# A circular 7x7 convolution kernel: pixel transfers of the head merged and reordered, forward jobs by halves, two weight jobs ahead of the first round

## The chip, the cores and the metric

The kernel runs on one core of a Trainium2 chip. The metric is the time of one execution on the device in microseconds (us); the median of several runs counts. TensorE (PE in the profile) multiplies matrices, PEld is its weight load, VectorE is DVE, ScalarE is ACT, GpSimd is POOL, and SyncE (SP) issues most of the DMA transfers.

## The reference

```python
x: (1, 224, 224, 96) bfloat16, w: (7, 7, 96, 96) bfloat16
wp = jnp.pad(w, ((0, H - K), (0, W - K), (0, 0), (0, 0)))
Xf = jnp.fft.rfft2(x.astype(jnp.float32), axes=(1, 2))
Wf = jnp.fft.rfft2(wp.astype(jnp.float32), axes=(0, 1))
Yf = jnp.einsum('bhwi,hwio->bhwo', Xf, Wf)
y = jnp.fft.irfft2(Yf, s=(H, W), axes=(1, 2)).astype(jnp.bfloat16)
```

This is a circular convolution over the image: each output pixel depends on its own row and the 6 above it and on its own column and the 6 to the left of it, wrapping around at the edges, and all 96 channels mix.

## The kernel before

The kernel cuts the image's 224 rows into 8 strips of 28 and takes each strip, with the 6 rows above it, through a short real transform over its rows; the result stands in 17 slots (`NS = 17`) of two numbers each. Along the columns it works directly, with seven taps shared between even and odd pixels. Four strips, with 6 rows above them, make a row block of 118 rows (`R = HB + PAD`); there are two row blocks, `jg` 0 and 1. The columns are cut into 7 tiles of 32 pixels.

The stages are these:

- Weights. `wqx` holds the weights with the taps on partitions. `prep_jobs(gi)` transforms one group of slots (`PGRP`) in 12 jobs of four matmuls each; each job fills a PSUM bank and is evicted into `WF`. Group 0 covers slots 0 and 1, group 1 slots 2 to 4; after its 12 jobs follow three VectorE differences (`diff`), so group 1 has 15 jobs.
- Forward. `f_jobs(t, s0, s1)` transforms the pixels of tile `t` for slots `s0` to `s1`. For the first eight slots of tile 0 there are four jobs for each row block: pixels 0 to 15, even and odd, then pixels 16 to 31, even and odd. Each job is eight matmuls of 64 columns into one bank, evicted as 512 columns into `xf`. The six wrap-around pixels at the right edge of the image (`xh_bufs`) go through `a_bank`, three matmuls of 136 columns a job.
- Rounds. `jit` forms sums and differences of `xf` on VectorE (the planes `J`), and `b_round(t, s, mid, end, ...)` multiplies them with `WF`. Inside a round, `mid` and `end` run waiting jobs of the queues `qs` (weights of later groups, forward jobs of later slots and tiles). `add(a, b, jobs)` spreads a list of jobs evenly over the half-rounds `a` to `b`, and `pace` says how many are due.
- The back transform of the output comes later and is not touched.

`evac` chooses the engine of each eviction by a planner: two running sums, `load["v"]` for VectorE and `load["a"]` for ScalarE, with an estimated cost for each eviction; the one with the smaller sum takes it. Just before the first round the sums are set to `BIAS` = 2000 and 0.

All engines run their instructions in the order in which the program issues them (`_Ordered`). SyncE's order in the head is six weight transfers, then ten pixel transfers: for each row block the wrap-around pixels (112 rows, then the 6 rows above, which wrap around), and then for each row block the pixels of tile 0 in three parts: first half of 112 rows, all pixels of the 6 wrap rows, second half of 112 rows. The first half is `TW * C + 32` = 1568 elements wide. The buffers lie in the last eight slots of `WF` (`late`), so that the profile shows these transfers as `WF<-in_x_dram`.

In program order the head is: group 0 of the weights, wrap-around pixels of both row blocks, eight forward jobs, the second tile's pixel transfers (which wait for the eviction of the fifth of the eight jobs, `last[-4]`), `jit(0, 0)`, and the rounds.

Of the kernel before, what the change touches and what calls it, by code (L numbers as in the profile page):

```python
# [21 lines left out]
PAD = KT - 1  # L22
Q = 2 * LC
MAGIC = 12582912.0
TW = 16
# [7 lines left out]
PGRP = ((0, 2), (2, 5), (5, 8), (8, 11), (11, 14), (14, 17))  # L33
# [11 lines left out]
MERGE = ()  # L45
NP2 = 0
FI = 6
LROUND = {8: 16, 11: 15}
WARM0 = 2
YLATE = {(0, 3): 0, (0, 4): 1}  # L50
BIAS = 2000.0


def slot(s, part):
    return part if s == 0 else 2 + 3 * (s - 1) + part
# [3 lines left out]
def kernel(  # L59
# [7 lines left out]
    _, H, W, C = x.shape  # L67
# [3 lines left out]
    HB = JG * B  # L71
    R = HB + PAD
# [36 lines left out]
    def bank():  # L109
        return pools["psb"].tile([128, 512], F32, name="pb")  # L110

    load = {"v": 0.0, "a": 0.0}
# [3 lines left out]
    def apart(key, zone, r):  # L116
        for z, q in parts.setdefault(key, []):
            if z != zone and q.engine != r.ins.engine:
                tc.declare_no_dep(r.ins, q, reason="disjoint parts of one tile")
        parts[key].append((zone, r.ins))  # L120
        return r

    def evac(out_ap, in_ap, n):
        if tail[0]:
            return tail_evac(out_ap, in_ap, n)
        cv, ca = 180 + 1.0 * n, 160 + 0.85 * n
        if load["v"] + cv <= load["a"] + ca:
            load["v"] += cv
            return VE.tensor_copy(out=out_ap, in_=in_ap)
        load["a"] += ca  # L130
        return SE.copy(out=out_ap, in_=in_ap)
# [5 lines left out]
    def dma(out_ap, in_ap):  # L137
        return DE.dma_start(out=out_ap, in_=in_ap)
# [11 lines left out]
    XW = 2 * TW * C  # L150
# [11 lines left out]
    XHW = PAD * C + 32  # L162
    late = WF[0:R, NSLOT - 8:NSLOT].rearrange("p a t o -> p (a t o)")
    x0_bufs = [late[:, i * (XW + 32):(i + 1) * (XW + 32)] for i in range(2)]
    xh_bufs = [late[:, 2 * (XW + 32) + i * XHW:2 * (XW + 32) + (i + 1) * XHW] for i in range(2)]
    assert 2 * (XW + 32 + XHW) <= 8 * NTAP * C and NSLOT - 8 > slot(PGRP[-1][0], 0)

    def load_rows(xb, jg, w0, npx, cut=0):
        h0 = jg * HB - PAD
        n = npx * C  # L170

        def ld(p0, p1, hh, c0=0, c1=n):
            return dma(xb[p0:p1, c0:c1], x[0, hh:hh + (p1 - p0), w0:w0 + npx, :].rearrange("h w c -> h (w c)")[:, c0:c1])
        if cut:
            return ld(PAD, R, h0 + PAD, 0, cut), ld(0, PAD, h0 % H), ld(PAD, R, h0 + PAD, cut, n)
        return ld(PAD, R, h0 + PAD), ld(0, PAD, h0 % H)
# [13 lines left out]
    def apart_w(r, rows=None, cols=None):  # L190
        for pr, pc, d in beside:
            if cols is not None and pc is not None and cols != pc or rows is None or pr is None or not rows & pr:
                tc.declare_no_dep(r.ins, d.ins, reason="other columns or rows")
        beside.append((rows, cols, r))
# [4 lines left out]
    for c, (c0, c1) in enumerate(cuts):  # L199
        apart_w(dma(wqx[up:up + lr, c0:c1], wsrc[0:lr, c0:c1]), {1, 2}, c)  # L200
        apart_w(dma(wqx[QD:up, c0:c1], wsrc[lr + QD - up + 1:lr + 1, c0:c1]), {-1}, c)
    for jg in range(2):
        load_rows(xh_bufs[jg], jg, W - PAD, PAD)
    for jg in range(2):
        load_rows(x0_bufs[jg], jg, 0, 2 * TW, TW * C + 32)

    def shift(eng, q, c):
        o, i = halves((q + 2) % 4, c, 0), halves(q, c, C2)
# [7 lines left out]
    def warm(n):  # L216
        pwu = bank()
        for _ in range(n):
            TE.matmul(pwu[:].rearrange("p (a b) -> p a b", a=4), lhsT=wu[:, 0:128], rhs=wur, start=True, stop=True)
# [62 lines left out]
    for h, r, lo, hi in ((0, 0, up - 1, up - 1 + PW - 1), (1, 0, 0, QD - 1), (1, 1, 2 * QD + up - 1, PW2 - 1)):  # L282
        o = flag[:, h, r:r + 1]
# [31 lines left out]
    for r, n, v in ((0, 0, 1.0), (0, LC, -1.0), (1, 1, -1.0), (1, L - 1, 1.0)):  # L315
        o = mf[:, :, 2 * NS - 2 + r:2 * NS - 1 + r]
# [71 lines left out]
    def prep_jobs(gi):  # L388
        s0, s1 = PGRP[gi]
        ns = s1 - s0  # L390
        full = gi == 0
        ncol = (NSLOT_OF(s0, s1) if full else 2 * ns) * NTAP
        nb = C // NB
        hb = NB // 2
        nr = 512 // NB if full else ncol
        assert ncol <= nr and NB * nr <= 512 and C2 % hb == 0

        def mk_(ob):
            def f():
                pw = bank()  # L400
                pv_ = pw[:, 0:NB * nr].rearrange("p (k h q) -> p k h q", h=2, q=nr)
                ev = Em[:, :, slot(s0, 0):slot(s1 - 1, 2) + 1, :]
                ev = Em.rearrange("p h a t -> p h (a t)")[:, :, 0:nr] if full else ev.rearrange("p h (s r) t -> p h s (r t)", r=3)[:, :, :, 0:2 * NTAP]
                for k in range(hb):
                    o = ob * hb + k
                    TE.matmul(pv_[:, k], lhsT=wqx[0:PW2, o:o + 127 * C + 1:C], rhs=ev, start=True, stop=True)
                pv_ = pv_[0:C]
                o0, o1 = ob * hb, (ob + 1) * hb
                wv = WF[0:C, slot(s0, 0):slot(s1 - 1, 2) + 1]
                if full:  # L410
                    wv = wv.rearrange("i a t (h o) -> i (a t) h o", h=2)
                    apart(("W", gi), ob, evac(wv[..., o0:o1], pv_[..., 0:ncol].rearrange("i k h q -> i q h k"), NB * ncol))
                    return
                wv = wv.rearrange("i (s r) t (h o) -> i s (r t) h o", r=3, h=2)
                apart(("W", gi), ob, evac(wv[:, :, 0:2 * NTAP, :, o0:o1],
                      pv_.rearrange("i k h (s q) -> i s q h k", s=ns), NB * ncol))
            return f

        def diff(s):
            def f():  # L420
                load["v"] += 60 + C * NTAP / 1.92
                w0, w1, w2 = (WF[0:C, slot(s, r)].rearrange("i t o -> i (t o)") for r in range(3))
                VE.tensor_tensor(out=w2, in0=w0, in1=w1, op=ALU.subtract)
            return f
        return [mk_(ob) for ob in range(nb)] + ([] if full else [diff(s) for s in range(s0, s1) if s not in REAL])

    def NSLOT_OF(s0, s1):
        return slot(s1 - 1, 2) + 1 - slot(s0, 0)
# [67 lines left out]
    def f_jobs(t, s0, s1):  # L496
        n = 2 * (s1 - s0) * JG
        nr = -(-TW * n // 512)
        e = [-(-TW * i // nr) for i in range(nr + 1)]
        assert max(b - a for a, b in zip(e[:-1], e[1:])) * n <= 512  # L500
        fv = Fm[:, :, s0:s1].rearrange("p r s j -> p r (s j)")

        def mk_(jg, a, b, ph):
            def f():
                pa = bank()
                for k in range(b - a):
                    i = 2 * (a + k) + ph
                    TE.matmul(pa[:, k * n:(k + 1) * n], lhsT=xbuf(t, jg)[:, i * C:i * C + 128], rhs=fv, start=True, stop=True)
                xo = xf_tiles[t][0:C, ph, :, s0:s1, HALO + a:HALO + b, jg * JG:(jg + 1) * JG]
                pi = pa[0:C, 0:(b - a) * n].rearrange("c (w r s j) -> c r s w j", r=2, s=s1 - s0, w=b - a)  # L510
                return apart(("A", t), (a, jg, ph, s0), evac(xo, pi, (b - a) * n))
            return f
        return [[mk_(jg, a, b, ph) for a, b in zip(e[:-1], e[1:]) for ph in range(2)] for jg in range(2)]
# [307 lines left out]
        for f in a_bank(0, xf0, xh_bufs[jg], 0, 3, jg, 0):  # L821
            f()
    fj = [f_jobs(0, a, b) for a, b in zip(FR0[:-1], FR0[1:])]
    last = [f() for jg in range(2) for f in fj[0][jg]]
    for jg in range(2):
        for d in load_x(1, jg):
            tc.add_manual_dep(d.ins, last[-4].ins.name, SYNC, reason="second tile's pixels later")
# [17 lines left out]
    def fills(qs, k):  # L845
        def f():
            for q in qs:
                pace(q, k)
        return f
# [3 lines left out]
    def add(a, b, jobs):  # L853
        qs.append([a, b, jobs, len(jobs)])

    for gi in range(1, len(PGRP)):
        add(2 * PGRP[gi - 1][0], 2 * PGRP[gi - 1][1] - 1, prep_jobs(gi))
    for t in range(2):
        scr_tiles[t] = dr_pool.tile([TW, NJ, NS, 4 * C], BF16, name="scr")
    bursts = {}  # L860
# [8 lines left out]
    for r in range(NS + LAG):  # L869
# [5 lines left out]
        for p in range(3):  # L875
            if r == (1, 3, 5)[p]:
# [4 lines left out]
                fj = f_jobs(1, SH2[p], SH2[p + 1])  # L881
# [4 lines left out]
        for s0, s1, k0, n in FR2:  # L886
            if 2 * r == k0:
                new_xf(2, s0, s1)
                fj = f_jobs(2, s0, s1)
# [33 lines left out]
    for t in range(2, NT):  # L923
# [19 lines left out]
        for s in range(NS):  # L943
# [8 lines left out]
            mid = fills(qs, 2 * s)  # L952
            if t == TL and s in LROUND:
                now = late_planes(LROUND[s])
            if t == TL and s >= SA:
# [18 lines left out]
    def first(j, h):  # L974
        pc = bank()[0:MO, 0:NC]
        TE.matmul(pc.rearrange("p (w g e) -> p w g e", w=2, e=4), lhsT=GA, rhs=TA[:, 2 * h:2 * h + 2, j], start=True, stop=False)
        return pc
# [7 lines left out]
    warm(WARM0)  # L985
    live = {k: first(*k) for k in order[:FI]}
    LF = 4
    for i, (j, h) in enumerate(order):
# [3 lines left out]
        k = i + 8 - LF  # L992
        if FI <= k < len(order):
            live[order[k]] = first(*order[k])
        if i % 2 == 1:
            w0 = TL * 2 * TW
# [34 lines left out]
```

## Time and profile before

| what | us |
|---|---|
| median of 3 runs (lowest to highest) | 256.68 (256.66 to 256.75) |
| profiled execution, whole time | 257.48 |
| its span, first to last instruction | 255.8 |
| TensorE busy in the span | 246.6 |
| VectorE, ScalarE, GpSimd busy | 215.1, 201.1, 107.9 |
| first matmul of the first round (slot 0) | 16.51 after the span's start |

The granted clock of TensorE is 0.994 of full speed. All times inside the profile are from the span's start. A line of the timeline has start, length, engine, source line, operation, output and inputs, shapes, the number of instructions merged, and in brackets the idle time before it with what ended it. All instructions carry line 92, a helper that records them, so groups are told apart by their tiles and shapes.

### The profile page before, as it was taken

The numbers are of one execution on the slowest core, as the hardware profiler recorded it, in microseconds if no ns is written. First come the engines' busy times: TensorE is split into PE (matmuls) and PEld (weight loads), VectorE is DVE, ScalarE is ACT, GpSimd is POOL, SyncE is SP. The second block draws the span as 40 slices with busy tenths as digits, with TensorE's granted clock in tenths as the row PEclk, the third lists the DMA queues.
The fourth block names the chain that finished last, engine by engine and source line by source line (L and its number), as shares of the span: only waits on it lengthen the run. The fifth ranks groups of instructions, "written<-read, shape, count | busy, mean of one in ns | idle before, by whom it ended". The sixth has DMA issues, their size and how long they took to land.

```text
span 255.8 us, 11924 instructions
## 1 busy us (share of the span) xinstructions
PE 246.6 (96%) x5015; PEld 231.7 (91%) x5015; DVE 215.1 (84%) x463; ACT 201.1 (79%) x499; POOL 107.9 (42%) x174
## 2 busy tenths in 40 slices
PE   8989999999999999999999999999999999999981
PEld 3779999999999999998999989999999999999971
DVE  6999899899888878789688896788978889989881
ACT  7889978484965977987988879988897976567762
POOL 7874514364447535331433324433233332465620
PEclk9999999999999999999999999999999999999997
DMA  7954002811111589997969379697959943595145
GB/s 169 239 155 128 27 26 68 255 42 57 49 49 53 160 221 150 279 318 211 311 172 265 96 202 246 180 266 194 329 203 209 265 160 104 146 176 164 54 128 171
DMA packets 41511, 42.80 MB, mean 167 GB/s; under 512 B 30836, under 2 KB 33072, under 8 KB 41458
## 3 DMA queue, kind: packets, MB, share of 16 engines
q1 hardware_dynamic: 41140, 41.36, 59.1%
q8 instruction: 39, 0.64, 1.1%
q0 software_dynamic: 192, 0.52, 0.7%
q10 hardware_dynamic: 126, 0.17, 0.2%
q14 instruction: 14, 0.11, 0.1%
HBM read 22.37 MB, written 19.66 MB: 164 GB/s over the span
## 4 chain that ended last, share of the span: by engine, by line
PE 87%; DMA 5%; ACT 2%; issue 2%; DVE 1%; SPq 1%; POOL 0%; DVEq 0%
PE pb L92 87%; DMA WF<-in_x_dram 2%; DMA wq<-in_w_dram 2%; SPq L92 1%; ACT xf L92 1%; DVE xf L92 1%; POOL yf L92 0%; ACT tt L92 0%; DVE u L92 0%; DVE v L92 0%; ACT WF L92 0%; ACT ct L92 0%; ACT tt__688 L92 0%; DVEq L92 0%
## 5 line engine op out<-in xcount | busy, mean ns | idle before, releaser
L92 PE MATMUL pb<-WF,J 96*128 96x96 bf16 x2782 | 160.8, 206 | 0.1
L92 PEld LDWEIGHTS <-J 96*128 96x128 bf16 x2782 | 137.0, 98 | 7.0 <-issue 0.2
L92 POOL TENSOR_TENSOR yf<-v,u 128x384 bf16<-128x384 f32 x70 | 69.7, 1010 | 119.6 <-issue 63.2
L92 ACT CAST xf<-pb 96x408 bf16<-96x408 f32 (+8 forms) x145 | 68.1, 492 | 3.8 <-PE pb L92 1.9
L92 PE MATMUL pb<-WF,xf 96*128 96x96 bf16 x991 | 61.5, 206 | 0.9 <-ACT xf L92 0.4
L92 DVE TENSOR_TENSOR J<-xf 96x1824 bf16<-96x1824 bf16 (+1 forms) x82 | 56.0, 722 | 0.1
L92 PEld LDWEIGHTS <-xf 96*128 96x128 bf16 x991 | 48.9, 98 | 1.6 <-issue 0.7
L92 PE MATMUL pb<-Fm,xn 118*128 118x136 bf16 (+5 forms) x576 | 44.4, 203 | 0.2 <-DVE u L92 0.2
L92 PE MATMUL pb<-tt,Gm 102*84 102x384 bf16 (+1 forms) x132 | 32.0, 325 | 0.0
L92 ACT CAST yo<-pb 84x384 bf16<-84x384 f32 (+1 forms) x65 | 27.8, 485 | 2.8 <-PE pb L92 2.8
L92 ACT CAST WF<-pb 96x480 bf16<-96x480 f32 (+1 forms) x59 | 29.2, 575 | 0.9 <-PE pb L92 0.9
L92 PEld LDWEIGHTS <-xn 118*128 118x128 bf16 x576 | 29.0, 97 | 0.5 <-issue 0.3
L92 ACT CAST J<-pb 84x384 bf16<-84x384 f32 (+1 forms) x65 | 28.0, 484 | 1.6 <-PE pb L92 1.6
L92 DVE TENSOR_TENSOR J<-J 96x912 bf16<-96x912 bf16 (+2 forms) x41 | 22.6, 552 | 0.0
L92 PE MATMUL pb<-wq 128*128 128x120 bf16 (+1 forms) x288 | 21.7, 226 | 0.0
L92 PEld LDWEIGHTS <-wq 128*128 128x128 bf16 x288 | 19.7, 149 | 0.6 <-ACT wq L92 0.5
L92 POOL TENSOR_TENSOR xn<-v,u 128x384 bf16<-128x384 f32 x12 | 10.9, 922 | 8.7 <-DVE J L92 5.7
L92 DVE TENSOR_TENSOR yf<-v,u 128x384 bf16<-128x384 f32 x20 | 11.3, 567 | 0.7
L92 PEld LDWEIGHTS <-Gm 102*84 102x84 bf16 (+1 forms) x132 | 11.4, 118 | 0.2
L92 ACT COPY xf<-xf 96x816 bf16<-96x816 bf16 (+4 forms) x16 | 10.0, 683 | 0.0
L92 PE MATMUL pb<-wu 128*128 128x512 bf16 x26 | 8.7, 509 | 1.1 <-DVE ct L92 1.1
L92 DVE TENSOR_TENSOR WF<-WF 96x960 bf16<-96x960 bf16 x14 | 9.2, 706 | 0.1
(410 smaller groups left out, 255.4 us busy)
## 6 DMA issues: line engine op xcount, KB each, us to landing
scr<-yf SPq DMA_DIRECT2D x30, 288.0 KB
xn<-in_x_dram SPq DMA_DIRECT2D x12, 672.0 KB
tt<-scr SPq DMA_DIRECT2D x24, 336.0 KB
out_dram<-yo SPq DMA_DIRECT2D x12, 252.0 KB
out_dram<-J SPq DMA_DIRECT2D x12, 252.0 KB
tt<-scr SPq DMA_DIRECT2D x6, 288.0 KB
scr<-yf SPq DMA_DIRECT2D x6, 192.0 KB
WF<-in_x_dram SPq DMA_DIRECT2D x2, 343.0 KB
```

Source lines behind the costliest of these rows:

```text
L92: r = fn(*a, **k)
```

## The change

There are three parts.

- Transfers. `load_both` loads the 112 rows of both row blocks in one transfer, `load_top` the six wrap rows of one row block. The new order behind the weights is: wrap-around pixels of both blocks; first halves of both blocks; wrap rows of the wrap-around pixels for block 0, for block 1; second half of block 0; wrap rows of tile 0 for block 0, for block 1; second half of block 1. That is eight transfers in the place of ten, with the same bytes.
- Forward jobs. The eight jobs run first half of block 0, first half of block 1, second half of block 0, second half of block 1.
- Weights. The first `NF = 2` jobs of group 1 run right behind the eight forward jobs, ahead of the first round; `load["v"]` is raised by `2 * BIAS` before them, so that the planner gives their evictions to ScalarE. The other 13 jobs of the group are spread as the 15 were.

```diff
+NF = 2
...
+    def load_both(o, n, w0, npx, c0, c1):
+        dma(late[PAD:, o:o + 2 * n].rearrange("p (j n) -> p j n", j=2)[:, :, c0:c1],
+            x[0, :, w0:w0 + npx, :].rearrange("(j p) w c -> p j (w c)", j=2)[:, :, c0:c1])
+
+    def load_top(xb, jg, w0, npx):
+        hh = (jg * HB - PAD) % H
+        dma(xb[0:PAD, 0:npx * C], x[0, hh:hh + PAD, w0:w0 + npx, :].rearrange("h w c -> h (w c)"))
+
+    XC = TW * C + 32
+    load_both(2 * (XW + 32), XHW, W - PAD, PAD, 0, PAD * C)
+    load_both(0, XW + 32, 0, 2 * TW, 0, XC)
     for jg in range(2):
-        load_rows(xh_bufs[jg], jg, W - PAD, PAD)
+        load_top(xh_bufs[jg], jg, W - PAD, PAD)
+    dma(x0_bufs[0][PAD:R, XC:XW], x[0, 0:HB, 0:2 * TW, :].rearrange("h w c -> h (w c)")[:, XC:XW])
     for jg in range(2):
-        load_rows(x0_bufs[jg], jg, 0, 2 * TW, TW * C + 32)
+        load_top(x0_bufs[jg], jg, 0, 2 * TW)
+    dma(x0_bufs[1][PAD:R, XC:XW], x[0, HB:2 * HB, 0:2 * TW, :].rearrange("h w c -> h (w c)")[:, XC:XW])
...
-    last = [f() for jg in range(2) for f in fj[0][jg]]
+    last = [f() for a in range(2) for jg in range(2) for f in fj[0][jg][2 * a:2 * a + 2]]
+    pj1 = prep_jobs(1)
+    load["v"] += 2 * BIAS
+    for f in pj1[:NF]:
+        f()
...
-        add(2 * PGRP[gi - 1][0], 2 * PGRP[gi - 1][1] - 1, prep_jobs(gi))
+        add(2 * PGRP[gi - 1][0], 2 * PGRP[gi - 1][1] - 1, prep_jobs(gi) if gi > 1 else pj1[NF:])
```

## The prediction

> **What bounds the kernel now.** I read the page first, then the chain of waits, then the timeline of the first 35 us by engine, then the busy time by stretch. Page, busy time and share of the span:
>
> ```profile
> PE 246.6 (96%) x5015; PEld 231.7 (91%) x5015; DVE 215.1 (84%) x463; ACT 201.1 (79%) x499; POOL 107.9 (42%) x174
> ```
>
> TensorE is the bound, and what lies ahead of its steady work is worth its full length. The chain of waits (start, length, what) shows that head:
>
> ```profile
> 2.65 5.33 DMA wq<-in_w_dram
> ...
> 9.20 6.18 DMA WF<-in_x_dram
> ...
> 15.43 0.42 PE pb L92 x8
> ...
> 15.87 0.59 ACT xf L92
> 16.46 0.05 issue
> 16.51 6.80 PE pb L92 x141
> ...
> 32.88 31.26 PE pb L92 x721
> ```
>
> The last pixel transfer lands at 15.38, eight matmuls and one ScalarE eviction follow, and round 0 starts at 16.51. Behind it the list of waits up to 45 us has nothing for TensorE but 0.2 us ahead of one weight load. So the end moves by what round 0's start moves, plus work taken out behind it, less any new waits. The weight-load timeline (start, length, form, idle before) shows where the pixels are waited for:
>
> ```profile
> 14.66 0.53 PEld L92 LDWEIGHTS <-WF 118*128 118x128 bf16 x16 [0.73 <-DMA WF<-in_x_dram]
> 15.42 0.52 PEld L92 LDWEIGHTS <-WF 118*128 118x128 bf16 x16 [0.23 <-DMA WF<-in_x_dram]
> 16.50 0.37 PEld L92 LDWEIGHTS <-xf 96*128 96x128 bf16 x8 [0.56 <-ACT xf L92]
> ```
>
> Row block 0 is done by 14.05 without a wait; block 1 waits 0.73 for its first half and wrap rows, 0.23 for its second half, and round 0 waits 0.56 for the last eviction. The stretches (us, busy of PE, PEld, DVE, ACT, POOL, clock, DMA share, GB/s) show a hole in the transfers:
>
> ```profile
> 8.00:9.00 1.00, 1.00 (x6) 0.35 (x4) 0.97 (x3) 0.87 (x1) 0.93 (x3) 1.00 0.90 276
> 9.00:10.00 1.00, 0.96 (x13) 0.79 (x13) 0.91 (x3) 0.28 (x1) 0.91 (x11) 1.00 0.74 163
> 10.00:11.00 1.00, 1.00 (x20) 1.00 (x18) 1.00 (x3) 0.99 (x3) 0.71 (x4) 1.00 0.83 227
> 11.00:12.00 1.00, 1.00 (x20) 1.00 (x19) 0.84 (x3) 1.00 (x4) 0.70 (x4) 1.00 1.08 288
> 12.00:13.00 1.00, 1.00 (x21) 1.00 (x20) 1.00 (x3) 1.00 (x3) 0.75 (x5) 1.00 0.97 239
> ```
>
> **The transfers.** SP's issues carry eight semaphores in turn, so the ninth transfer waits for the first to land, and so on: the ten pixel transfers issue at 3.58, 4.04, 4.89, 5.32, 6.77, 7.18, 8.00, 8.36, 8.83 and 9.20 (0.27 to 0.43 each), the third to seventh right behind a landing of weights. Their last landing marks are 8.50, 8.71, 9.04, 9.29, 10.68, 11.08 (block 0's wrap rows), 12.98, 14.44, 14.55 (block 1's wrap rows), 15.38: the order of issue. After the change there are eight: both wrap-pixel blocks (252 KB), both first halves (686 KB, now seen at 4.04 and not at 6.77), two wrap-row transfers of the wrap pixels, second half of block 0, wrap rows of blocks 0 and 1, second half of block 1, whose issue falls in the place of 8.36. The two issues saved (0.7 us) are off the path: SP's next work waits until 15.72 for an eviction. The bytes stay, 1722 kB.
>
> All is now queued before it is needed, so the hole closes: against 268 (mean of the three full stretches) 9 to 11 us lost 105 + 41 = 146 kB, 0.54 us. The last half then lands at 15.38 - 0.54 = 14.84.
>
> But block 0's wrap rows, needed by every first-half job, now end at 1348 kB of the queue (132.75 x 2 + 343 x 2 + 329 + 36 KB of 1024) instead of 660. Call their landing T. At 9.0 us 560 kB had started; the other 788 take 2.94 at 268, so their last packet starts at 11.94. From there to the landing: in the trace block 0's wrap rows landed 1.47 after the byte count reached them (9.61 to 11.08), the 343 KB that ends at the same 1348 kB landed 1.98 after (12.46 to 14.44). T is 13.4 by the nearer row (the same transfer) and 13.9 by the farther. I take 13.4. A merged half completes only with both blocks, which costs nothing here, since T is later. The wrap-pixel jobs need their wrap rows at 12.24; those end at 974 kB, 10.5 + 1.5 = 12.0, and a slip there hides before T.
>
> The Trainium skill (DMA: Bandwidth & Descriptors, Anatomy of one DMA) gives every transfer, however small, a fixed cost of about 2.0 us, most of it the receipt of its last write. As an estimate from that figure T would be 11.94 + 2.0 = 13.9 and the gain 0.1; the two rows above, 1.47 and 1.98, lie below it and at it.
>
> **The jobs.** The eight jobs come in the order first halves of both blocks, then second halves; their evictions stay VectorE, ScalarE, ScalarE, VectorE, S, V, S, V (the planner's sums do not depend on the order). A job is eight matmuls, 0.26 (16 in 0.53); results 0.18 after the last; ScalarE takes 512 columns every 0.47 (24.16 to 24.63), 0.58 to the end. Round 0's first convolution needs the seventh job's eviction, ScalarE's fourth:
> - from T: 0.05 + 0.53 + 0.18 + 3 x 0.47 + 0.58 + 0.05 = T + 2.80 = 16.20;
> - from the last half: 0.05 + 0.26 + 0.18 + 0.58 + 0.05 = 14.84 + 1.12 = 15.96. (The same sum gives 15.38 + 1.12 = 16.50 for the kernel before; it shows 16.51.)
>
> The later counts: 16.51 - 16.20 = 0.31 gained. VectorE, 0.60 apart, ends its fourth at T + 3.2 = 16.6 (now 16.79), so the planes for the next convolution are not late. Before the change evictions of block 0 ran while block 1 was still coming; now all eight are bunched behind T, and that is why an earlier last half gives only part of its 0.54.
>
> **Two weight jobs ahead of round 0.** Eight 120-column matmuls (20 took 1.26 at 16.86, 0.063 each), 0.50 in all, go from behind round 0's start into the wait for ScalarE: TensorE's last pixel job ends at 15.5, the two jobs at 16.0, before 16.20. Their banks are those of the first two pixel jobs, free by 14.9. If that cover were gone (T later delays job and eviction alike, so the wait stays) they would cost their 0.50 again, no more than now. Both evictions are forced onto ScalarE, 0.445 each (17.33, 17.78, 18.24), 0.89. In its queue they stand ahead of round 0's copy (17.06) and the next four weight evictions. It has idle time of 0.61 before 17.06 and 0.29 before 21.72 to take them, but is then busy without a break to 30 us, and returns banks late: TensorE's 26.43 starts as a weight eviction of 25.84 ends. Thirteen jobs remain of fifteen, paced 5, 4, 4 and not 5, 5, 5; following the planner's sums, seven evictions change engine up to 29 us and none in the next 30 us; ScalarE has one weight eviction more up to 23 us. Walking the three queues with these rows, TensorE is 0.81 ahead at 26 us and waits 0.21 more for banks at 27 to 28. So 0.50 - 0.21 = 0.29 stays; bounds 0 (all turned to bank waits) and 0.50.
>
> The second tile's loads hang on the fifth eviction, 15.7 in both cases; first used at 23.32, they land at 21.1, so 0.6 earlier use is covered by 2.2.
>
> **Sum.** 0.31 + 0.29 = 0.60. The profiled execution took 257.48 (span 255.8 and 1.7 around it) and would take 256.88; the median of the runs shown, 256.68, lies 0.80 below the profiled one: 256.08, say 256.1. Each us of T is one us, and the sum is zero at T = 14.0. A measurement tells some 0.2%, 0.51 us, from no change.
>
> **Rivals.**
> - *The transfers gain, T does not.* T = 13.9 by the farther row: gain 0.10, 256.6. For it: exactly the same packets stand ahead on each engine as ahead of the mark at 14.44, and a landing is that of the slowest engine. Against: the hole of 146 kB closes for them too. 0.25.
> - *The wrap rows come last and decide, slower.* If the rate is that of 9 to 11 us (195), T = 9.0 + 4.04 + 1.98 = 15.0, round 0 at 17.8: 1.0 lost, 257.7. It decides from T = 14.0, is measurable from 14.5. For it: every first-half job now hangs on a transfer that moved from behind 623 kB to behind 1311. Against: 239 to 288 when fed. 0.18.
> - *Better than that*: with the lag of 1.3 that block 0's first half shows (9.4 to 10.68) at 288, T = 13.0, round 0 starts at 15.8, and with 0.50 kept the gain is 1.2: 255.5. It lies on the forecast's side, 0.1.
> - *The change doesn't do what it says.* The Trainium skill (same page, Why a DMA increments its semaphore by 16 and not by 1) lets the slowest dimension set how many engines share a transfer. If the two blocks were that dimension, 686 KB would run on two of 16, 30 GB/s at 239 for all: some 17 us more, 273. Against: each 8 by 112 read-back transfer of the trace shows 16 landing marks. 0.02.
>
> Forecast 0.45, with its own range 255.8 to 256.4. Faster by over 0.2%: most of the forecast (0.40) and the better case, 0.50. Within 0.2%: the rest of the forecast and the first rival, 0.30. Slower: the rivals on that side, 0.20. The range 255.4 to 257.1 reaches from the better case into the slower one and leaves 0.05 below and 0.15 above.
>
> **What would show it.** No weight load waits between 14.05 and 16.5 as now; instead one wait for pixels at 12.9 that ends at T (13.4), then 32 matmuls without a gap, eight weight matmuls, and round 0 at 16.2. DMA share near 1 at 9 to 11 us. ScalarE without its 0.61 hole. Wrong would be: a weight load released after 14.0, round 0 after 16.8, or waits for ScalarE at 23 to 30 us that eat more than 0.5.

## The result and the profile after

The change makes the kernel slower: 257.34 us (256.89 to 257.72) against 256.64 (256.47 to 256.96), a ratio of 1.0025 [1.0017, 1.0034]. A second set of runs gave 1.0024 [1.0009, 1.0038]. Both intervals lie above 1; the loss is a quarter of a percent. The prediction had 256.1.

The profiled execution of the changed kernel took 257.39 (span 255.7 and 1.7 around it). The profiled execution of the kernel before took 257.48, so two profiles of equal length stand beside medians that differ by 0.70. A second profile of the kernel before (e1 below) has a span of 254.8. It is the fairer partner, and both are used in what follows. In the changed kernel the helper that records all instructions stands at line 93.

The page after, busy time and share of the span:

```profile
PE 244.9 (96%) x5015; PEld 231.2 (90%) x5015; DVE 214.6 (84%) x462; ACT 201.1 (79%) x500; POOL 108.0 (42%) x174
```

The chain of waits of the changed kernel (start, length, what) has its one long wait for pixels on a transfer that was issued at 7.18, the wrap rows of block 0:

```profile
7.18 7.14 DMA WF<-in_x_dram
14.32 0.05 issue
14.36 0.66 PE pb L93 x16
15.02 0.02 issue
15.04 2.06 ACT xf L93 x4
17.10 0.05 issue
17.14 6.28 PE pb L93 x133
```

Before, this chain went through the last half of block 1. Now the last half is in time and the wrap rows (14.32) are not: sixteen matmuls and four ScalarE evictions follow them, and round 0 starts at 17.14. The weight-load timeline (start, length, form, number, idle before) says the same:

```profile
14.36 1.92 PEld L93 LDWEIGHTS <-WF 118*128 118x128 bf16 x64 [1.61 <-DMA WF<-in_x_dram]
16.21 0.58 PEld L93 LDWEIGHTS <-wq 128*128 128x128 bf16 x8
17.14 0.37 PEld L93 LDWEIGHTS <-xf 96*128 96x128 bf16 x8 [0.35 <-ACT xf L93]
```

All 64 forward matmuls run without a break behind one wait of 1.61. Before, half of them were done by 14.05. The stretches after (us, busy of PE, PEld, DVE, ACT, POOL, clock, DMA share, GB/s):

```profile
9.00:10.00 1.00, 0.96 (x16) 0.99 (x17) 0.54 (x2) 0.49 (x1) 0.90 (x12) 1.00 1.06 273
10.00:11.00 1.00, 1.00 (x20) 1.00 (x19) 1.00 (x3) 0.98 (x3) 0.69 (x4) 1.00 1.01 258
11.00:12.00 1.00, 1.00 (x20) 1.00 (x18) 1.00 (x3) 1.00 (x3) 0.75 (x4) 1.00 1.09 280
12.00:13.00 1.00, 0.93 (x16) 0.74 (x13) 1.00 (x3) 1.00 (x3) 0.75 (x5) 1.00 1.01 199
13.00:14.00 1.00, 0.00 (x0) 0.00 (x0) 0.59 (x2) 0.51 (x2) 0.74 (x4) 1.00 0.47 84
14.00:15.00 1.00, 0.64 (x22) 0.64 (x23) 0.19 (x1) 0.00 (x0) 0.73 (x5) 1.00 0.10 38
15.00:16.00 1.00, 1.00 (x41) 1.00 (x37) 0.99 (x2) 0.96 (x3) 0.69 (x5) 1.00 0.09 16
```

The hole at 9 to 11 us is closed, as predicted, and another one has opened at 13 to 16: the last 138 kB come at a DMA share of 0.47, 0.10 and 0.09. The same stretches of the kernel before, in its second profile (e1):

```profile
9.00:10.00 1.00, 1.00 (x17) 0.96 (x16) 0.69 (x2) 0.51 (x2) 0.84 (x12) 1.00 0.76 176
10.00:11.00 1.00, 1.00 (x19) 1.00 (x18) 1.00 (x4) 0.98 (x3) 0.75 (x4) 1.00 1.02 294
...
12.00:13.00 1.00, 1.00 (x26) 1.00 (x25) 1.00 (x4) 1.00 (x4) 0.77 (x4) 1.00 0.99 265
13.00:14.00 1.00, 0.80 (x28) 0.67 (x24) 1.00 (x3) 1.00 (x4) 0.71 (x4) 1.00 0.30 101
14.00:15.00 1.00, 0.79 (x27) 0.82 (x28) 0.81 (x3) 0.81 (x2) 0.75 (x4) 1.00 0.00 0
```

Here the hole is there, but one us long (0.76, 176 GB/s, then 294), nothing moves after 14, and the last half lands at 14.63, where the changed kernel has 15.30. From 12 to 13 the engines are as busy as in the changed kernel (0.99 and 1.01) and move 265 GB/s, not 199.

### The profile page after: what moved, and what is told of

The parts are those of the page before. It is cut to its first block, busy times and chain, and to the rows that moved or that the text cites. A ratio compares the mean times of both kernels' runs of the same rounds, so it can differ in the third digit from the quotient of the medians.

```text
span 255.7 us, 11919 instructions
## 1 busy us (share of the span) xinstructions
PE 244.9 (96%) x5015; PEld 231.2 (90%) x5015; DVE 214.6 (84%) x462; ACT 201.1 (79%) x500; POOL 108.0 (42%) x174
## 4 chain that ended last, share of the span: by engine, by line
PE 84%; DMA 6%; ACT 2%; issue 2%; SPq 2%; DVE 1%; POOL 0%; DVEq 0%
PE pb L93 84%; DMA WF<-in_x_dram 3%; DMA wq<-in_w_dram 2%; SPq L93 2%; ACT xf L93 1%; DMA out_dram<-J 1%; DVE xf L93 1%; POOL yf L93 0%; ACT tt L93 0%; DVE u L93 0%; DVE v L93 0%; ACT WF L93 0%; ACT tt__4426 L93 0%; ACT ct L93 0%; ACT tt__686 L93 0%
## 5 line engine op out<-in xcount | busy, mean ns | idle before, releaser
L93 POOL TENSOR_TENSOR yf<-v,u 128x384 bf16<-128x384 f32 x70 | 69.0, 1000 | 119.2 <-issue 64.0
L93 ACT CAST xf<-pb 96x408 bf16<-96x408 f32 (+6 forms) x146 | 68.4, 491 | 4.6 <-PE pb L93 2.5
L93 DVE CAST xf<-pb 96x512 bf16<-96x512 f32 (+4 forms) x14 | 8.3, 615 | 1.2 <-PE pb L93 1.2
```

What stands on the lines that cost most here:

```text
L93: r = fn(*a, **k)
```

## Seventeen profiles in one table

All times are us from the start of the profiled span. A landing mark is one record of a transfer's semaphore being raised; a transfer has landed with its last mark. Columns two to four are the last marks of the wrap rows of tile 0 and of the last half. "By the rule" is the latest of: wrap rows of block 0 + 2.80, wrap rows of block 1 + 2.18 (both only where the jobs run by halves), last half + 1.12. The 2.80 and 1.12 are the prediction's sums; the 2.18 was put at 2.2 to 2.3 ahead of e10 and is e10's value. Ratios are of all runs of a kernel against the runs of the kernel before that were taken beside them. The landings are of one profiled execution each, which need not lie at the median: those of e5, e6 and e7 were the fastest of theirs.

| kernel | block 0 | block 1 | last half | by the rule | round 0 | ratio |
|---|---|---|---|---|---|---|
| before, shown above | 11.08 | 14.55 | 15.38 | 16.50 | 16.51 | |
| e1 before again | 10.91 | 14.08 | 14.63 | 15.75 | 15.76 | 0.9998 [0.9989, 1.0007] |
| e3 weight jobs only | 10.93 | 13.85 | 14.52 | 15.64 | 15.66 | 0.998 [0.9968, 0.9991] |
| e8 three weight jobs | 10.99 | 14.02 | 14.99 | 16.11 | 16.29 | 0.9984 [0.9974, 0.9994] |
| e10 order, weight jobs | 11.22 | 14.47 | 15.20 | 16.65 | 16.65 | 0.9987 [0.9975, 0.9999] |
| after | 14.32 | 14.61 | 15.30 | 17.12 | 17.14 | 1.0025 [1.0017, 1.0034] |
| e11 after again | 14.23 | 14.50 | 15.21 | 17.03 | 17.06 | 1.0024 [1.0009, 1.0038] |
| e2 no weight jobs | 14.12 | 14.63 | 15.16 | 16.92 | 16.93 | 1.0047 [1.0035, 1.006] |
| e5 unmerged | 13.71 | 14.19 | 14.83 | 16.51 | 16.61 | 1.0008 [0.9999, 1.0018] |
| e14 x0 unmerged | 14.18 | 14.45 | 15.08 | 16.98 | 17.00 | 1.001 [0.9995, 1.0025] |
| e15 xh unmerged | 14.43 | 14.63 | 15.37 | 17.23 | 17.33 | 1.0016 [1.0003, 1.003] |
| e17 xh wraps up | 14.04 | 14.37 | 15.13 | 16.84 | 16.94 | 1.0024 [1.0016, 1.0033] |
| e13 one transfer moved | 12.49 | 14.09 | 14.97 | 16.27 | 16.19 | 0.9989 [0.9975, 1.0002] |
| e6 wraps first | 10.36 | 10.65 | 14.73 | 15.85 | 15.96 | 0.9998 [0.9988, 1.0008] |
| e7 wraps apart | 9.91 | 12.49 | 14.47 | 15.59 | 15.61 | 0.9979 [0.997, 0.9989] |
| e12 apart, unmerged | 9.96 | 12.96 | 14.89 | 16.01 | 16.03 | 0.9969 [0.9956, 0.9983] |
| e16 apart, no weight jobs | 10.12 | 12.98 | 15.00 | 16.12 | 16.13 | 1.0009 [0.9995, 1.0024] |

Not in the table are e4, where another transfer decided, e18, whose TensorE clock fell, and e9, whose profiled execution ran at a granted clock of 0.56 (409 us) and says nothing on the question; e16 is the same kernel again.

One more number holds in all these traces. From round 0's first matmul over 200 matmuls of the rounds (those that read `xf` or `J`) it is 21.71 to 21.75 without weight jobs ahead (the kernel before twice, e2, e16), 21.12 to 21.19 with two, and 20.93 with three. From there to the end it is 217.2 to 217.6, in e8 alone 217.9. So the time of a profiled execution is round 0's start + 240.3 with two jobs (21.15 + 217.45 + 1.7), and 0.58 more without. What any of these kernels gains or loses is in round 0's start, in those 0.58, and, in e8, in what the third job costs later.

## The experiments

**Both halves of the change.** e1 is the kernel before again. e2 is the changed kernel without its weight jobs:

```diff
-NF = 2
+NF = 0
```

> The kernel before, once more. Its profiled execution took 257.48, while its eight timed runs have a median of 256.64; the changed kernel's profiled execution (257.39) is like its median (257.34). Theory A (the changed kernel is slower because block 0's wrap rows land at 14.32, and the profile of before that the sum was made against was some 0.8 longer than usual in the head): the ratio is 1.000, and a fresh profile has its span near 255.0 and round 0's first matmul at 15.6 to 16.0, not 16.51. Rival B (the two weight jobs on ScalarE's queue are what costs): the head of a fresh profile again has round 0 at 16.5, and the 0.8 lies elsewhere in the span.

> The changed kernel with NF = 0: transfers and job order as changed, no weight job ahead of round 0. Theory A: the wrap rows still land at about 14.3, round 0 starts at T + 2.8 = 17.1 as with the jobs, and the 0.50 us of weight matmuls go back behind it, so it is slower than the changed kernel by 0.3 to 0.5 (257.7 to 257.8; ratio to before 1.004). Rival B: without the two evictions on ScalarE the loss against before vanishes (256.6).

e3 is the kernel before, with its transfers and its order of forward jobs, and only the weight jobs of the change:

```diff
+NF = 2
...
+    pj1 = prep_jobs(1)
+    load["v"] += 2 * BIAS
+    for f in pj1[:NF]:
+        f()
...
+        add(..., prep_jobs(gi) if gi > 1 else pj1[NF:])
```

> The kernel before with nothing but the two weight jobs ahead of round 0; its ten transfers and its job order stay. Theory A: round 0 starts where it does in the kernel before, and 0.3 to 0.5 us of matmuls leave the path behind it: 256.2 to 256.4, ratio 0.9985. Rival B: slower than before, 256.9 to 257.3.

e1 came at 256.54 us, e2 at 257.86, e3 at 256.28, each close to its theory A. The weight jobs are a gain in both surroundings: e3 against before 0.2%, the changed kernel against e2 0.22% (1.0047 to 1.0025, measured at two times). The rest of the change, e2 against e1, is a loss of 1.3 us. e3 beats both kernels of the case.

**Wrap rows earlier, all four together.** e4 puts tile 0's wrap rows right behind the merged first halves, and with that the two small wrap transfers behind them:

```diff
     load_both(0, XW + 32, 0, 2 * TW, 0, XC)
+    for jg in range(2):
+        load_top(x0_bufs[jg], jg, 0, 2 * TW)
     for jg in range(2):
         load_top(xh_bufs[jg], jg, W - PAD, PAD)
```

> The changed kernel with one thing moved: the wrap rows of tile 0 (two transfers) go right behind the merged first halves, ahead of the wrap-around pixels' wrap rows and of block 0's second half. Theory A: T falls from 14.3 to about 12.2, the last half (15.3 in the changed kernel) decides, round 0 starts at 15.3 + 1.12 = 16.4, 0.7 earlier than in the changed kernel: 256.6, and the weight load shows two shorter waits in the place of one of 1.61. Rival B: T falls too, but the time stays within 0.2 of the changed kernel's 257.34.

A miss for both theories: 257.70 (1.0043). Four six-row transfers in a row landed at 13.19, 13.59, 13.84 and 14.08, each later behind its bytes than the one ahead. (The lag of a transfer, here and below, is the time from the moment when the count of pixel bytes whose packets have started reaches its end in the queue to its last landing mark: 2.76, 3.01, 3.25 and 3.45 us.). The small ones, which TensorE needs first, became the wait (1.96, ending at 13.88), and round 0 started at 17.38.

**Merged or not, first or apart.** e5 issues every transfer of both blocks as two, in the changed order:

```diff
-    load_both(2 * (XW + 32), XHW, W - PAD, PAD, 0, PAD * C)
-    load_both(0, XW + 32, 0, 2 * TW, 0, XC)
+    for jg in range(2):
+        dma(xh_bufs[jg][PAD:R, 0:PAD * C], x[0, jg * HB:(jg + 1) * HB, W - PAD:W, :]...)
+    dma(x0_bufs[0][PAD:R, 0:XC], x[0, 0:HB, 0:2 * TW, :]...)
+    dma(x0_bufs[1][PAD:R, 0:XC], x[0, HB:2 * HB, 0:2 * TW, :]...)
```

e6 moves all four wrap transfers behind the first of the wrap-around pixels:

```diff
-    load_both(0, XW + 32, 0, 2 * TW, 0, XC)
     for jg in range(2):
         load_top(xh_bufs[jg], jg, W - PAD, PAD)
+    load_top(x0_bufs[0], 0, 0, 2 * TW)
+    load_top(x0_bufs[1], 1, 0, 2 * TW)
+    load_both(0, XW + 32, 0, 2 * TW, 0, XC)
     dma(x0_bufs[0][PAD:R, XC:XW], ...)
-    for jg in range(2):
-        load_top(x0_bufs[jg], jg, 0, 2 * TW)
```

e7 takes tile 0's two wrap transfers apart, one ahead of the merged first halves and one behind:

```diff
-    load_both(0, XW + 32, 0, 2 * TW, 0, XC)
     for jg in range(2):
         load_top(xh_bufs[jg], jg, W - PAD, PAD)
+    load_top(x0_bufs[0], 0, 0, 2 * TW)
+    load_both(0, XW + 32, 0, 2 * TW, 0, XC)
+    load_top(x0_bufs[1], 1, 0, 2 * TW)
     dma(x0_bufs[0][PAD:R, XC:XW], ...)
-    for jg in range(2):
-        load_top(x0_bufs[jg], jg, 0, 2 * TW)
```

> The changed kernel with its order of the head's rows and its two weight jobs, but with every transfer of both row blocks issued as two transfers, one for each block, as in the kernel before. Theory W (the two transfers of x0's wrap-around rows stand back to back late in the queue, their 6144-byte packets and the packets behind them run slowly, so the last half and both wrap landings come late): nothing that matters is changed, the last half of x0 lands at about 15.2 us, block 0's wrap rows at 14.1 or later, round 0 starts at 16.9 or later, and the time is 257.2 to 257.4 us. Theory M (the merged transfers themselves, a form of descriptor that covers both blocks, or the closed hole in the issues, are the cause): last half at 14.6, block 0's wrap rows at about 13.6, round 0 at about 16.4, time 256.5 to 256.7 us.

> The changed kernel with merged transfers, all four wrap-around transfers right behind the first one of xh (xh both, xh wraps, x0 wraps, x0's first halves, x0's second halves). Nothing is left for the first jobs to wait for but x0's halves. If the landing of block 0's wrap rows is what decides (and the last half lands as early as in the kernel before, 14.6 us), round 0 starts 1.1 us behind the last half, at 15.8, and the time is about 256.1 us. Theory W: four slow transfers in a row slow what is behind them, the last half lands at 15.2 to 15.3 us, round 0 starts at 16.3 to 16.4, time about 256.6 us.

> The changed kernel with merged transfers and the two transfers of x0's wrap-around rows taken apart: block 0's ahead of x0's first halves, block 1's behind them, then the second halves. Theory W (six-row transfers back to back are the cause): each now runs alone, the last half lands at 14.6 to 14.8 us, round 0 starts at about 15.8, time about 256.2 us. Theory M (the merged transfers are the cause): last half at about 15.2, round 0 at 16.3, about 256.7 us.

e5 lies between its two theories (257.04; wrap rows at 13.71, round 0 at 16.61). e6 came at 256.87, above both of its numbers; its profile, with the last half at 14.73 and round 0 at 15.96, is that of the fastest of eleven executions (256.27). e7 does what the first of its theories says: 256.39, last half at 14.47. In the weight-load timeline of e7 the wait for the wrap rows is gone, and the short one that is left is for the last half:

```profile
12.91 1.19 PEld L93 LDWEIGHTS <-WF 118*128 118x128 bf16 x37
14.51 0.52 PEld L93 LDWEIGHTS <-WF 118*128 118x128 bf16 x16 [0.41 <-DMA WF<-in_x_dram]
14.97 0.57 PEld L93 LDWEIGHTS <-wq 128*128 128x128 bf16 x8
15.61 0.37 PEld L93 LDWEIGHTS <-xf 96*128 96x128 bf16 x8
```

With the same merged transfers and the same weight jobs as the changed kernel, and all wrap rows elsewhere in the queue, round 0 starts 1.53 earlier in these two profiles. By the rule 0.70 of it is the gate that is gone (17.12 to 15.30 + 1.12), the rest is the earlier last half. The profiled execution of e7 (256.08) was the fastest of nine; the medians lie 0.95 apart.

**A third weight job.** e8 is e3 with one job more:

```diff
-NF = 2
+NF = 3
```

> The kernel before with three jobs of the second weight group taken out of round 0's list and put behind the forward jobs; transfers and forward jobs as before. Two jobs gave 0.4 us. If ScalarE has room for a third job before the sum of round 0 needs it, each job is worth about 0.2 us more: 256.0 to 256.2 us. Rival: the third job makes ScalarE late for its share of the transposes, and the time is that of two jobs or more, 256.3 us or above.

The rival: 256.50, ratio 0.9984 where two jobs gave 0.998. The timeline of TensorE shows why: waits for ScalarE and VectorE take back what the job gave (20.93 against 21.15 over the first 200 matmuls of the rounds, but 25.24 against 24.85 over the next 400). The traces of e3 and of the changed kernel have no such wait there.

```profile
25.71 0.76 PE L93 MATMUL pb<-WF,J 96*128 96x96 bf16 x14 [0.38 <-ACT WF L93]
39.69 0.95 PE L93 MATMUL pb<-Fm,xn 118*128 118x32 bf16 x32 [0.36 <-DVE u L93]
```

**Transfers alone, order alone, and both again.** e9 and e16 are e7 with `NF = 0`, the edit of e2. e10 is e3 with the changed order of forward jobs:

```diff
-    last = [f() for jg in range(2) for f in fj[0][jg]]
+    last = [f() for a in range(2) for jg in range(2) for f in fj[0][jg][2 * a:2 * a + 2]]
```

e11 is the changed kernel again. e12 is e7 with ten unmerged transfers, by the edit of e5.

> The changed kernel with x0's wrap-around transfers taken apart as in the run that did so, and no job of the second weight group ahead of round 0. Theory: a transfer order whose wrap rows are early leaves the bytes to set the landing of the last half (14.5 us, as in the kernel before), so the merged transfers and the closed hole give nothing by themselves, and the time is that of the kernel before, 256.6 to 256.9 us. Rival: the closed hole is worth the 0.3 us that the prediction gave it, and the time is 256.3 to 256.4 us.

> The kernel with x0's wrap rows apart and no weight jobs ahead again, for its profile. If the transfers by themselves give nothing: last half at 14.5 to 14.9, round 0 at 15.6 to 16.0 as in the kernel before, and after it the waits for banks and J of the kernel before (0.1 to 0.2 us each at 26 to 33 us); 256.7 to 257.0 us.

> The transfers of the kernel before, with the forward jobs by halves and two weight jobs behind them. Block 1's wrap rows land at 14.1 us and by halves they gate the third of eight forward jobs, where by blocks they gate the fifth. Block 0's wrap rows were followed by round 0 after 2.8 us with all eight jobs to do; with six left I put it at 2.2 to 2.3, so round 0 at about 16.3 where two jobs alone had 15.7, part of it recovered later: time 256.6 to 256.8 us. Rival: the order of the jobs costs nothing, because the last half decides in any case: 256.2 to 256.4 us.

> The changed kernel again, beside the others of this call. Theory: block 0's wrap rows land at 13.8 to 14.4 us, round 0 starts 2.8 us behind that, and the time is 257.2 to 257.4 us. If the late landing was an accident of one profile, the landing is at 13.4 and the time stays at 257.3, which would leave the loss without its cause.

> x0's wrap-around transfers taken apart, with ten unmerged transfers and two weight jobs. The unmerged form of the changed kernel was 0.3 us faster than the changed kernel. If merging costs only by way of the landing of the wrap rows, which are now early, nothing changes: last half at 14.5 us, round 0 at 15.6, 256.4 us. If the merged transfers cost by themselves: 256.1 us. If the later issue of ten transfers counts: last half at 14.8, 256.6 us.

e9 and e16 came at 257.25 and 257.24, above the 256.6 to 257.0 that was expected, but beside a kernel before of 256.94 and 256.89: ratios of 1.0012 [0.9997, 1.0026] and 1.0009 [0.9995, 1.0024]. With wrap rows in a good place the merged transfers and the closed hole give nothing, rather a little less. e16's landings are just behind the expected ones (last half 15.00, round 0 at 16.13). So what e7 gains on the kernel before is the weight jobs'. e10 came at 256.59, at the lower edge of what was expected, with round 0 at 16.65, later than expected. By halves, block 1's wrap rows gate the third job, and the weight loads wait for them at 14.47:

```profile
14.57 1.47 PEld L93 LDWEIGHTS <-WF 118*128 118x128 bf16 x48 [1.28 <-DMA WF<-in_x_dram]
...
16.65 0.37 PEld L93 LDWEIGHTS <-xf 96*128 96x128 bf16 x8
```

The 48 loads are the six jobs left. That the order costs time shows in this trace alone: the interval of e10's ratio overlaps e3's. e11 repeats the loss (257.46) and the late landing (14.23). e12 is the best version found, 256.30 and 0.9969, but its interval overlaps those of e7 and e3, and no run tells the three apart.

**What makes the wrap rows late.** e13 moves one transfer of the changed kernel, block 0's wrap rows, ahead of block 0's second half:

```diff
+    load_top(x0_bufs[0], 0, 0, 2 * TW)
     dma(x0_bufs[0][PAD:R, XC:XW], ...)
-    for jg in range(2):
-        load_top(x0_bufs[jg], jg, 0, 2 * TW)
+    load_top(x0_bufs[1], 1, 0, 2 * TW)
```

e14 and e15 undo one merge each (of e5's edit, only the lines of `x0_bufs`, and only those of `xh_bufs`). e17 moves the two small wrap transfers ahead of the merged first halves:

```diff
-    load_both(0, XW + 32, 0, 2 * TW, 0, XC)
     for jg in range(2):
         load_top(xh_bufs[jg], jg, W - PAD, PAD)
+    load_both(0, XW + 32, 0, 2 * TW, 0, XC)
```

In e18 ScalarE issues tile 0's wrap rows at its start:

```diff
     for jg in range(2):
-        load_top(x0_bufs[jg], jg, 0, 2 * TW)
+        load_top(x0_bufs[jg], jg, 0, 2 * TW, SE)
```

> The changed kernel with one transfer moved: block 0's wrap rows of x0 go ahead of block 0's second half. So far every run has round 0 at the latest of three: block 0's wrap rows + 2.80, block 1's wrap rows + 2.18 (they gate the third of eight jobs), last half + 1.12. The 337 kB that are moved behind are 1.2 us at the 0.28 MB/us of this stretch, so block 0's rows land at about 13.0, block 1's stay at 14.4 to 14.6 and decide: round 0 at 16.6 to 16.8 where the changed kernel has 17.1, 256.9 to 257.1 us. Rival: only the last half decides, or the jobs' order has no gate of its own: round 0 at 16.3, 256.6 us.

> The changed kernel with x0's first halves in two transfers (xh stays merged). If the merge of x0's first halves is what makes one engine's queue run behind the others, and with it the landing of block 0's wrap rows: that landing at 13.7, round 0 at 16.6, 257.0 us. If the merge of xh, or both: 14.2, 17.0, 257.3 us.

> The changed kernel with xh in two transfers (x0's first halves stay merged), the counterpart: 14.2, 17.0 and 257.3 us if the merge of x0's first halves costs; 13.7, 16.6 and 257.0 us if that of xh does. If both runs give 257.3, the 0.3 us of the unmerged kernel are no effect of merging.

> The changed kernel with the two small wrap transfers (of the wrap-around pixels) moved ahead of x0's first halves; x0's wrap rows stay where they are, behind block 0's second half, with the same bytes ahead of them. If six-row transfers close together pile up their lag: with the bulk of x0's first halves between the two pairs, the lag of block 0's wrap rows falls from 2.5 to about 2.0, they land at 13.7 to 13.8, round 0 starts at 16.6 and the time is about 256.9 us. If only the place in the queue counts: 14.2, 17.0, 257.3 us.

> The changed kernel with x0's two wrap-row transfers issued by ScalarE at the very start, on a queue of its own, so that they land long before they are needed. Then the last half alone sets round 0: it lands at 14.5 to 15.0 as the bytes have it, round 0 at 15.6 to 16.1, 256.0 to 256.5 us. Rival: the 74 KB are now ahead of the weights and delay everything behind them, or the early issue delays ScalarE's first work: 256.7 us or more.

e13, one line moved, turns the loss into 256.61, ratio 0.9989 [0.9975, 1.0002]. Block 0's rows landed at 12.49 and block 1's at 14.09, 0.3 to 0.5 earlier than I had put them. The weight loads wait for the latter, as expected, but the time is the rival's number:

```profile
14.13 1.46 PEld L93 LDWEIGHTS <-WF 118*128 118x128 bf16 x48 [0.80 <-DMA WF<-in_x_dram]
```

And the stream does not slow down from 12 to 13 as in the changed kernel:

```profile
12.00:13.00 1.00, 1.00 (x24) 1.00 (x23) 1.00 (x3) 1.00 (x3) 0.77 (x4) 1.00 1.06 263
```

e14 (257.20) and e15 (257.37) left the landing at 14.18 and 14.43, and e17 (257.35) at 14.04: neither merge by itself makes the rows late, and the small wrap transfers ahead of them explain 0.3 at most. Their place in the queue does, as e13 shows; but in its new place the transfer also no longer stands next to block 1's wrap rows, and e13 does not separate the two. Whether merging costs a little besides is open: the unmerged e5 landed at 13.71, but the intervals of e5, e14, e15 and the changed kernel overlap.

e18 was no clean test. The wrap rows were out of the way by 7 us, but the second weight transfer, ahead of which they now went, landed at 6.71 where e7 has 5.35. In the profiled execution, TensorE had nothing to do for 2.25, and its granted clock fell. The clock is the number ahead of the last two of each line:

```profile
9.00:10.00 1.00, 0.00 (x0) 0.00 (x0) 0.90 (x2) 1.00 (x1) 0.93 (x11) 1.00 1.01 254
10.00:11.00 1.00, 0.65 (x11) 0.68 (x12) 0.97 (x2) 0.38 (x2) 0.78 (x3) 1.00 1.04 250
11.00:12.00 1.00, 1.00 (x15) 1.00 (x14) 1.00 (x3) 0.79 (x2) 0.70 (x4) 0.66 1.03 240
12.00:13.00 1.00, 1.00 (x13) 1.00 (x11) 0.29 (x2) 0.91 (x2) 0.75 (x4) 0.50 1.04 244
...
14.00:15.00 1.00, 1.00 (x14) 1.00 (x13) 0.72 (x2) 0.51 (x2) 0.75 (x4) 0.63 0.22 71
```

There round 0 started at 18.27. This execution took 258.49; four of the twelve took 258.46 to 258.80, at a mean clock of 0.987 to 0.992, and the others 256.80 to 257.42, at 0.993 to 0.999. So the median of 257.38 (1.0032) has the rival's direction, but the profile shows the dearer kind of execution, and no profile shows what the others paid for.

## Why the prediction was wrong, step by step

**T = 13.4: the step that failed.** Block 0's wrap rows landed at 14.32, and both signs that were named for being wrong came: a weight load released after 14.0 (14.36) and round 0 after 16.8 (17.14). The byte count was right: 1348 kB had started by 11.80 (estimate 11.94). The lag behind it was not: 2.52 us, where the sum had 1.47. I had two rows, 1.47 and 1.98, and took the smaller because it belonged to the same transfer. That row was also misread. Its 9.61 goes by the mean rate of 9 to 10 us, 163 GB/s, but two thirds of the bytes of that us came in its first half: by the packet records 660 kB had started at 9.41, so the row is 1.67 and would have given T = 13.6. Over the runs, block 0's rows in their old place lag 1.45 to 1.73 (five profiles). In the old queue the two transfers that end at 1348 and 1385 kB lag 1.47 to 2.05. Block 0's rows in their new place, ending at 1348 kB, lag 2.07 to 2.59 (seven profiles). So the lag does not go with the transfer, and the true value lay outside both rows. The first rival's T of 13.9 was still too early; the slower rival (from T = 14.5 a measurable loss) had its mechanism right, the wrap rows deciding, with the wrong reason: up to 1348 kB the rate held (273, 258, 280 GB/s), and the lag did it.

The depth of the queue alone does not set the lag either. Block 1's wrap rows end at 1385 kB in the old queue, in e13 and in the changed order. Behind a transfer of 112 rows they lag 1.56 to 2.05 (old queue) and 2.01 (e13), right behind block 0's wrap rows 2.42 to 2.70 (seven profiles). And in e6, with four six-row transfers in a row near the head, block 0's rows lag 2.46 at 308 kB. So the neighbours count. No run has block 0's rows at 1348 kB without block 1's next to them, so how much of the 2.52 is depth and how much the neighbour stays open.

A reading that covers part of it, in numbers: a 112-row transfer leaves sixteen landing marks, a six-row one a mark right behind its issue (7.64) and six late ones, 12.98 to 14.32 for block 0's rows. So six engines share six rows. If they are always the same six, those carry 2 x 1152 + 2 x 6144 = 14.6 kB on top of 102.1 (7 rows a transfer, twice 1152 + 3136 + 3008); at 268 / 16 = 16.75 GB/s that is, at the end of the queue, 0.87 us more than the other ten. The byte count is a mean over sixteen, the landing that of the slowest. The tail fits too: a DMA share of 0.47, then 0.10, is that of a few engines still at work. But it does not explain why the lag grew: up to and with block 0's rows the surplus is 2 x 1152 + 6144 = 8.4 kB, 0.50 us, and it was the same in the old queue. The Trainium skill (DMA: Bandwidth & Descriptors, Why a DMA increments its semaphore by 16 and not by 1) says that a hardware-queue transfer over k engines takes the lowest-numbered k, and that the marks of the others are written at once. The marks agree with the second; no run here shows which engines worked.

What the packets do show is a slower stream where the two transfers stand side by side. In the seven profiles with the changed order at that place, the stream ran at 157 to 211 GB/s from 12 to 13 us, at a DMA share of 1.01 to 1.14, and packets of 3008 bytes took 0.23 to 0.34 us on average. In the nine with the two apart (the old queue, e7, e12, e13 and e16) it ran at 239 to 269, at a share of 0.94 to 1.07, and the packets took 0.17 to 0.20. In e4, with four in a row, two us ran at 119 and 112 GB/s. What slows the packets is not shown.

**The hole was not a loss.** The prediction closed 146 kB of hole and moved the last half by 0.54 to 14.84. The hole closed and the last half landed at 15.30 and 15.21. Part of the hole was that one profile's own: in e1 it is one us, some 90 kB short of 268. And what the changed kernel won it lost again where the stream slowed. By 12.0 us 1408 kB had started, 1379 in e1 and 1408 in e3; by 13.0 it was 1607, against 1628 and 1649. In kernels with the hole the last half landed at 14.52 to 15.38. e7, e12 and e16 fill 9 to 10 us (e7: 282 GB/s) but move only 172 to 225 from 8 to 9; they have 14.47 to 15.00. e13, which moves 217 or more in each us from 8 to 13, has 14.97. So no profile shows an earlier last half from a closed hole beyond the scatter.

**The base.** The profile that I subtracted from had its last half at 15.38, and its execution took 0.80 more than the median. I carried that difference through as a constant. But e1, the same kernel, has 14.63 for its last half and 15.76 for round 0, so 0.75 of it was in the very stretch that the change is about. Against the record profile round 0 lost 0.63 and the weight jobs gave 0.58 back, hence two equal profiles; against e1 it is 1.38 lost and 0.58 given, and a span longer by 0.85. From the medians round 0 starts at 15.76 in the kernel before (256.64 - 240.88) and at 17.04 in the changed one (257.34 - 240.3), so e1 is the profile nearer to the median.

**T + 2.80 and last half + 1.12: right.** The table holds to 0.1 in all rows but e8 (0.18 late) and e6 (0.11). The step said that each us of T is one us, and so it was: e13 and e7 got the time back by moving T. What it lacked is the gate of block 1's wrap rows, + 2.18, which the order by halves brings forward. In e10's trace, the one from which the 2.18 is taken, it costs 0.33 against the last half.

**Two weight jobs: right, mis-sized.** The gross 0.50 was to lose 0.21 to bank waits. It lost none; 0.58 was gained (21.73 - 21.15); why it is 0.08 more than the matmuls moved is open. With the third job the waits do come (0.38 and 0.36 above), so the give-back was real but began one job later.

**The other rivals.** The 686 KB transfer landed at 11.75 with sixteen marks from 10.94 on, no two-engine transfer. The better case fell with T. The Trainium skill's fixed cost of about 2.0 us (DMA: Bandwidth & Descriptors, Anatomy of one DMA), which that section fits to transfers that GpSimd issues, while SyncE issues these, had given an estimate of 13.9 for T. That was nearer than my 13.4, and the traces with this order and at least one merge show 14.04 to 14.43.

**The sum as it was.** Predicted were -0.31 and -0.29. The 0.70 between the medians is 1.28 lost ahead of round 0 (15.76 to 17.04 by the two constants) and 0.58 gained behind it.

## What to carry to other kernels

A transfer has landed with its last mark, and that can be 2.5 us behind its bytes. Small transfers on which much work waits belonged, here, apart from each other and ahead of large ones; the lag of one is to be read from a row with the same place and the same neighbours in the queue, not from the same transfer elsewhere. A dip in the mean rate is not time won by closing it, unless the stream stays at full rate behind it; read the count of started bytes at several times. And before a stretch of one profile is taken as the base of a sum, its own run should lie at the median; where it does not, the surplus may lie in that very stretch, as 0.75 of 0.80 did here. The same holds for the profile of an experiment.

## What was not expected of the hardware

- The landing of the last half scatters by 0.86 us between profiles of the same transfers (14.52 in e3, 15.38 in the kernel before). The time follows it one to one where nothing else decides, and single runs of the kernel before, taken together, spread from 256.3 to 257.5.
- Lags pile up where six-row transfers follow each other: 2.76, 3.01, 3.25, 3.45 in e4, and 2.09, 2.43, 2.46, 2.52 near the head of the queue in e6. The stream slows there with the engines still busy (119 and 112 GB/s at shares of 1.18 and 0.90 in e4).
- After 2.25 us without a matmul the granted clock fell to 0.50, after work had resumed (0.66 as the mean of 11 to 12 us), and was back at 1.00 by 15 us (e18, one profiled execution). A gap of 1.66 in e15 had no such effect (1.00 in each us behind it). The Trainium skill (TensorE: Matmul & The Clock Gate, What's actually happening) lets the clock drop after an idle window of about 3.4 us. Here a shorter gap sufficed.
